# Where the first x of an MLP is loaded and scaled during attention, in a fused attention and MLP kernel: six head pairs instead of five

## The chip, the cores and the metric

One core of a Trainium2 chip runs the whole kernel. The metric is device time in microseconds: 708.55 us is the median of three runs (708.1 to 709.25).

## The reference

Attention over 4 batches, 8 heads, 576 positions and head size 64, with a bias that a small network makes from the distance of two positions; then an MLP over the 2304 tokens with model size 512 and inner size 2048.

```python
scores = scale * np.matmul(q, k.transpose(0, 1, 3, 2))
psi_rel = np.log1p(np.abs(rel))                      # rel = i - j
psi_i = np.log1p(np.maximum(pos[:, None], 1.0))
x = (psi_rel / psi_i)[..., None]
h = np.maximum(x @ w1 + b1, 0.0)
scores = scores + (h @ w2).transpose(2, 0, 1)[None]
scores = scores - np.max(scores, axis=-1, keepdims=True)
attn = np.exp(scores)
attn = attn / (np.sum(attn, axis=-1, keepdims=True) + 1e-09)
x = np.matmul(attn, v)        # then (batch, position, head * size), 2304 x 512
h = x @ w_in
g = np.where(h > 0.0, h, np.exp(np.minimum(h, 0.0)) - 1.0)
out = g @ w_out
```

## The kernel before

The order of the instructions on each engine is written out by hand. There are three stages: the bias of all heads, attention, and the MLP.

**Attention** goes over 16 head pairs n (4 batches of 4 pairs). A pair has five units i = 0 to 4, for the query blocks u = 0, 1, 4, 2, 3 (`order`). In a unit TensorE makes the scores of both heads into two PSUM banks each (line 291, S in `STEPS`), VectorE adds the bias and takes the row minimum (line 303, X), ScalarE takes the exponential (line 314), TensorE transposes the result of the unit before (line 355, T), and two copies bring each transposed block to SBUF (line 359): the second copy (r = 1) is VectorE's for even u and ScalarE's for odd u. TensorE also makes the weighted sums of v of the pair before (line 399). They go out to DRAM unscaled (`xd`, lines 409 to 412). At the second unit of pairs 4, 8 and 12 the row sums of the batch before are inverted (lines 324 and 325), at the fourth they are transposed and sent to DRAM (`rd`, line 333).

All loads and stores of this stage are issued by SP in one queue in program order: the next pair's k and q at the end of unit 0 (lines 99 to 105), one raw block of MLP weights in unit 2 (line 250), v in unit 3 (line 111). Each pair also decodes one block of MLP weights, given as 64-bit floats: VectorE (lines 259, 263, 265) and GpSimd (lines 255, 268), stored at line 270. The first of these VectorE steps, line 259, comes once in each pair, in its second unit.

**The first x of the MLP.** `early` is a table of what else is done in the last pairs; its key (n - 16, i) names a pair and the unit at whose end it happens. `load_x(0, r, h)` fetches the weighted sums of half the channels (r) for 384 tokens (h) with `xd` DMAs (line 448) into `xr` and, for each, two DMAs that spread the inverted sums over partitions (line 452) into `rr`, which has one buffer: three DMAs where the tokens lie in one piece (h = 0), nine where they lie in three pieces (h = 1). `scale_x` multiplies the two on VectorE (line 460). `high_x` (line 483) and `low_x` (line 486) split the result into two parts for TensorE (B11, B12, B21, B22), `sums_x` (line 474) makes sums for the fast matrix product.

**The MLP** works on 3 blocks of 768 tokens; for each it goes over 8 blocks of the inner size. The first two (i = 0, 1) are plain products (`eight`), the others a seven-product scheme (`seven`) whose left operands are sums of the weights, made by `make_w(i)`. This generator's steps are placed by `at(i, k, ...)`, into the k-th product of block i. The second matmul (line 723) adds into six PSUM banks; when one is complete, VectorE or ScalarE copies it to an `os` tile (line 732, three buffers) and SP sends it out (line 734).

Of the kernel before, what the change touches and what calls it, by code (L numbers as in the profile page):

```python
# [10 lines left out]
F32 = mybir.dt.float32  # L11
# [13 lines left out]
def kernel(  # L25
# [11 lines left out]
    nc = tc.nc  # L37
    B, HP, D, _, S = qT.shape
    NT, DM = out.shape
    H = 2 * HP  # L40
    P = 128
# [37 lines left out]
    def w_bank(name):  # L79
        return wp.tile([P, 512], F32, tag="w", name=name)  # L80
# [8 lines left out]
    NP = len(pairs)  # L89
# [253 lines left out]
    def trans_p(n, u):  # L343
        pta, ptb = st["pt", n]

        ss = st["ss", n, u]
        if u < NCH:
            dst, o = (pta, u * P) if u < 2 else (ptb, (u - 2) * P)
            banks = [w_bank("wt") for r in range(2)]
            for x in range(2 * NCH):  # L350
                e, j = divmod(x, NCH)
                c = e * (S + TAIL) + j * P
                for r in range(2):
                    q = slice(r * TAIL, (r + 1) * TAIL)
                    nc.tensor.transpose(banks[r][:, x * TAIL:(x + 1) * TAIL], ss[q, c:c + P], ident[q, q])  # L355
            for r in range(2):
                d = dst[:, 0:2 * NCH, o + r * TAIL:o + (r + 1) * TAIL]
                copy = nc.vector.tensor_copy if r == 1 and u % 2 == 0 else nc.scalar.copy
                copy(d, banks[r].rearrange("p (x t) -> p x t", t=TAIL))
                yield  # L360
        else:
            o = 2 * P
            M = NCH * TAIL
            banks = [w_bank("wt") for e in range(2)]
            for j in range(NCH + 1):
                for e, w in enumerate(banks):
                    r = slice(e * TAIL, (e + 1) * TAIL)
                    if j < NCH:
                        c = j * P
                        nc.tensor.transpose(w[:, j * TAIL:(j + 1) * TAIL], ss[r, c:c + P], ident[r, r])  # L370
                    elif e == 0:
                        nc.tensor.transpose(w[r, M:M + TAIL], ss[r, NCH * P:], ident[r, r])
                    else:
                        nc.tensor.transpose(w[:, M:M + TAIL], ss[r, S - P:], ident[r, r])
            for e, w in enumerate(banks):
                r = slice(e * TAIL, (e + 1) * TAIL)
                d = pta[:, e * NCH:(e + 1) * NCH, o:o + TAIL]
                nc.scalar.copy(d, w[:, 0:M].rearrange("p (j t) -> p j t", j=NCH))
                nc.scalar.copy(pta[r, 2 * NCH, o:o + TAIL], w[r, M:M + TAIL])
                yield  # L380
# [123 lines left out]
    xo = dict(zip(("B11", "B12", "B21", "B22"), slots))  # L504
# [5 lines left out]
    def attention():  # L510
# [17 lines left out]

        V, G = nc.vector, nc.gpsimd
        early = {  # L530
            (-5, 3): [(load_x, 0, 0, 0)],
            (-4, 1): [(scale_x, 0, 0, 0, V)],
            (-4, 2): [(load_x, 0, 0, 1)],
            (-4, 4): [(scale_x, 0, 0, 1, V)],
            (-3, 0): [(load_x, 0, 1, 0)],
            (-3, 1): [(high_x, 0, "B11", xo["B11"], V.tensor_copy)],
            (-3, 2): [(scale_x, 0, 1, 0, V)],
            (-3, 3): [(load_x, 0, 1, 1), (low_x, 0, "B11", xo["B11"], V)],
            (-2, 0): [(scale_x, 0, 1, 1, V)],
            (-2, 1): [(high_x, 0, "B12", xo["B12"], V.tensor_copy)],  # L540
            (-2, 2): [(low_x, 0, "B12", xo["B12"], V)],
            (-2, 3): [(high_x, 0, "B21", xo["B21"], V.tensor_copy), (sums_x, 0, ("T1",), G)],
# [25 lines left out]
        for n in range(NP):  # L568
# [4 lines left out]
            for i, u in enumerate(order):  # L573
                run = scores(n, u)
                back = trans_p(n, order[i - 1]) if i > 0 else trans_p(n - 1, order[-1]) if n > 0 else iter(())
                for op in STEPS[i]:
                    if op in ("S", "X"):
# [40 lines left out]
        for _ in trans_p(NP - 1, order[-1]):  # L618
            pass
# [10 lines left out]
    def mlp():  # L630
        ep = ctx.enter_context(tc.tile_pool(name="ep", bufs=3))
# [17 lines left out]
        FIRST = 2  # L649
# [13 lines left out]
        def make_w(i):  # L663
            q = i % NQ
            ta, tb = place_w(i, 0), place_w(i, 1)
            S1 = wq.tile([P, 4, AW], F32, tag="S", name="S")
            wa, wb = wab.pop(2 * q), wab.pop(2 * q + 1)
            A11, A12, A21, A22 = (w[:, k * AW:(k + 1) * AW] for w in (wa, wb) for k in range(2))
            hi, lo = AT[i][:, 0], AT[i][:, 1]
            flat = lambda t: t.rearrange("p a m -> p (a m)")  # L670
            v = nc.vector
            parts = [
                (flat(hi[:, 4:6]), flat(lo[:, 4:6]), wa[:, 0:DM]),
                (W2[i][:, 0, 0], W2[i][:, 1, 0], wa[:, DM:]),
                (hi[:, 6], lo[:, 6], A22),
                (W2[i][:, 0, 1], W2[i][:, 1, 1], wb[:, DM:]),
                (flat(hi[:, 0:4]), flat(lo[:, 0:4]), flat(S1)),
            ]
            high = lambda k: nc.scalar.copy(parts[k][0], parts[k][2])
            low = lambda k: v.tensor_sub(parts[k][1], parts[k][2], parts[k][0].bitcast(F32))  # L680
            yield
            v.tensor_add(S1[:, 0], A21, A22)
            v.tensor_sub(S1[:, 2], A11, A21)
            high(0)
            yield
            v.tensor_sub(S1[:, 1], S1[:, 0], A11)
            v.tensor_sub(S1[:, 3], A12, S1[:, 1])
            low(0)
            yield
            high(4)  # L690
            yield
            low(4)
            high(2)
            yield
            low(2)
            high(1)
            yield
            high(3)
            yield
            low(1)  # L700
            yield
            low(3)
            yield
            nc.sync.dma_start(out=wA[q], in_=ta.bitcast(F32))
            nc.sync.dma_start(out=wB[q], in_=tb.bitcast(F32))
# [4 lines left out]
        def second(i, order):  # L710
            j = i // NQ
            for e, h in order:
                gh, gl = g[i, e]
                wh, wl = (
                    [ws[2 * i + e][f][:, DM:] for f in range(2)] if i < FIRST else [W2[i][:, f, e] for f in range(2)]
                )
                for t in range(3 * h, 3 * h + 3):
                    if (j, t) not in acc:
                        acc[j, t] = accp.tile([P, DM], F32, tag="acc", name="acc")
                        count[j, t] = 0  # L720
                    for x, w in ((gh, wh), (gh, wl), (gl, wh)):
                        count[j, t] += 1
                        nc.tensor.matmul(  # L723
                            acc[j, t],
                            lhsT=x[:, t * P:(t + 1) * P],
                            rhs=w,
                            start=(count[j, t] == 1),
                            stop=(count[j, t] == 6 * NQ),
                        )
                        if count[j, t] == 6 * NQ:  # L730
                            os = ep.tile([P, DM], F32, tag="os", name="os")
                            (nc.scalar.copy if t % 2 else nc.vector.tensor_copy)(os, acc[j, t])  # L732
                            t0 = 2 * j * HB + t * P
                            nc.sync.dma_start(out=out[t0:t0 + P, :], in_=os)
                        yield


# [98 lines left out]
        def at(i, k, fn, *args):  # L836
            plans.setdefault((i, k), []).append((fn, args))

        V, G = nc.vector, nc.gpsimd
# [11 lines left out]
        for i in range(FIRST, NQ + FIRST):  # L851
            q = i % NQ
            run = make_w(i)
            for e in range(2):
                at(i - 2, 0 if i - 2 < FIRST else 2, load_w, 2 * q + e, wq if i % 2 == 0 else keep)
            for k in (0, 1, 1, 2, 2, 3, 3) if i == FIRST else (0, 1, 2, 3, 4, 5, 6):
                at(i - 1, k, next, run)
            at(i, 0, next, run)
            at(i, 1, next, run)
            at(i, 3, next, run, None)  # L860
# [53 lines left out]
    with tc.manual_schedule():  # L914
        make_identity(nc, ident)
        bias_phase()
        attention()
        ph1.close()
        ps1.close()
        mlp()  # L920
# [58 lines left out]
```

## Time and profile before

| | |
|---|---|
| median of 3 runs | 708.55 us |
| the profiled execution, its own time | 708.4 us |
| its span, first to last instruction | 706.6 us |
| mean granted TensorE clock | 0.994 |
| TensorE matmul, busy | 679.3 us (96%) |
| VectorE, busy | 470.7 us (67%) |
| ScalarE, busy | 440.6 us (62%) |
| GpSimd, busy | 75.3 us (11%) |
| attention, first raw weights used to the MLP's first product | 68.75 to 319.47 us |

The engines are named PE (TensorE's matmuls), PEld (its weight loads), DVE (VectorE), ACT (ScalarE), POOL (GpSimd) and SP. Lines of a timeline begin with the start and the duration in microseconds; instructions of a kind that follow each other are merged, with their count behind an x. A bracket at the end tells how long the engine was idle before, and what ended it. The share of busy time is a mean over the three stages; what a change in one place is worth is read from the waits there.

### The profile page before, as it was taken

The page shows a single profiled execution, that of the slowest core. Times are in us where ns is not written, and L with a number is a line of the kernel's source. Part 1 is how long each engine was busy: PE and PEld are TensorE (multiplying, and loading weights), DVE is VectorE, ACT ScalarE, POOL GpSimd, SP SyncE. Part 2 cuts the span into 40 slices and gives each one's busy share as a digit, 9 for nine tenths or more (in the row PEclk, how much of TensorE's full clock was granted, in tenths as well). Part 3 has the DMA queues.
Part 4 walks back from the last instruction along what each step waited for, and adds up shares of the span by engine and source line. Part 5 has one row for each costly group of instructions (what it writes and reads, how often), then busy time and mean ns, then how long its engine had stood idle before and what let it go on. Part 6 is the DMA issues. An engine that isn't in the chain of part 4 may idle for free.

```text
span 706.6 us, 13181 instructions
## 1 busy us (share of the span) xinstructions
PE 679.3 (96%) x4992; PEld 508.7 (72%) x4992; DVE 470.7 (67%) x948; ACT 440.6 (62%) x953; POOL 75.3 (11%) x104
## 2 busy tenths in 40 slices
PE   5997999999999979899999999999999999999997
PEld 3434555555555545458799988999988899988896
DVE  6995767767766757875777899854456754444443
ACT  6996787787877757675665667643444644434433
POOL 0001332322233212330000000000000000000000
PEclk9999999999999999999999999999999999999999
DMA  6998655456555766625379977898684455555202
GB/s 165 222 221 210 219 176 200 159 163 205 185 187 185 222 175 195 216 103 187 81 268 333 330 260 257 317 350 310 212 306 176 164 209 212 202 207 214 88 1 89
DMA packets 49934, 144.58 MB, mean 205 GB/s; under 512 B 13376, under 2 KB 26448, under 8 KB 42192
## 3 DMA queue, kind: packets, MB, share of 16 engines
q1 hardware_dynamic: 49136, 143.44, 60.9%
q8 instruction: 39, 0.64, 0.4%
q10 hardware_dynamic: 736, 0.31, 0.2%
q14 instruction: 23, 0.19, 0.1%
HBM read 92.14 MB, written 40.97 MB: 188 GB/s over the span
## 4 chain that ended last, share of the span: by engine, by line
PE 51%; issue 1%; DVE 1%; ACT 1%; DMA 0%; SPq 0%; ACTq 0%
PE acc L723 27%; PE h L772 24%; DVE bias L497 0%; DMA out_dram<-os 0%; DVE e L751 0%; ACT e L758 0%; ACT gh L752 0%; DVE xs L486 0%; ACT bias L493 0%; DVE gl L746 0%; ACT e L757 0%; ACT xs L483 0%; DVE os L732 0%; DMA wf<-da 0%; ACT os L732 0%
## 5 line engine op out<-in xcount | busy, mean ns | idle before, releaser
L723 PE MATMUL acc<-wB,gh 128*128 128x512 f32 x528 | 171.3, 392 | 0.0
L303 DVE CUSTOM_DVE_ANT_0 ss<-ps,bias 128x576 f32<-128x576 f32 x128 | 91.8, 754 | 58.9 <-PE ps L291 50.2
L314 ACT ACTIVATE ss<-ss,nm 128x576 f32<-128x576 f32 x128 | 98.2, 769 | 36.9 <-DVE nm L303 36.4
L291 PE MATMUL ps<-kk,qq 64*128 64x288 f32 (+1 forms) x640 | 110.2, 423 | 7.9 <-DVE nm L303 7.6
L772 PE MATMUL h<-bias 128*128 128x384 f32 x552 | 111.8, 339 | 0.8 <-DVE rs L332 0.5
L723 PEld LDWEIGHTS acc<-wB,gh 128*128 128x128 f32 x528 | 98.1, 188 | 14.3
L772 PEld LDWEIGHTS h<-bias 128*128 128x128 f32 x552 | 99.6, 188 | 9.0 <-DVE e L751 1.9
L723 PE MATMUL acc<-wB,gl 128*128 128x512 f32 x264 | 103.8, 393 | 0.0
L291 PEld LDWEIGHTS ps<-kk,qq 64*128 64x128 f32 (+1 forms) x640 | 63.3, 178 | 28.2 <-DVE nm L303 12.5
L752 ACT CAST gh<-e 128x384 fp32r<-128x384 f32 x96 | 49.4, 514 | 44.8 <-DVE e L751 44.2
L757 ACT ACTIVATE e<-c 128x384 f32<-128x384 f32 x66 | 34.7, 525 | 53.4 <-DVE c L803 53.4
L746 DVE TENSOR_TENSOR gl<-e,gh 128x384 fp32r<-128x384 f32 x96 | 53.2, 554 | 18.1 <-ACT gh L752 15.8
L772 PE MATMUL h<-bias,wA 128*128 128x384 f32 x276 | 56.3, 338 | 0.9 <-issue 0.9
L751 DVE SCALAR_TENSOR_TENSOR e<-e,c 128x384 f32<-128x384 f32 x66 | 36.7, 557 | 30.1 <-ACT e L758 29.9
L757 ACT ACTIVATE e<-h 128x384 f32<-128x384 f32 x28 | 13.8, 491 | 68.3 <-PE h L772 68.3
L193 PE MATMUL bps<-rel,cs 128*32 128x288 f32 x576 | 45.5, 430 | 10.7 <-ACT rel L183 7.8
L723 PEld LDWEIGHTS acc<-wB,gl 128*128 128x128 f32 x264 | 49.5, 187 | 7.8
L399 PE MATMUL wv<-pta,vv 128*64 128x320 f32 (+1 forms) x320 | 54.4, 454 | 0.0
L772 PEld LDWEIGHTS h<-bias,wA 128*128 128x128 f32 x276 | 50.1, 188 | 5.0 <-issue 1.4
L758 ACT ACTIVATE e<-e 128x384 f32<-128x384 f32 x96 | 50.5, 526 | 3.0
L355 PEld LDWEIGHTS wt<-ident,ss 64*128 64x128 f32 x1024 | 37.5, 139 | 19.6 <-issue 13.0
L803 DVE TENSOR_TENSOR c<-h,u 128x384 f32<-128x384 f32 x66 | 36.7, 556 | 20.1 <-PE h L772 20.1
(105 smaller groups left out, 924.6 us busy)
## 6 DMA issues: line engine op xcount, KB each, us to landing
wB<-wB SPq DMA_DIRECT2D x22, 1024.0 KB, 5.0
raw<-in_wd_dram SPq DMA_DIRECT2D x16, 1024.0 KB, 11.0
bias<-wA SPq DMA_DIRECT2D x9, 1792.0 KB
wA<-wA SPq DMA_DIRECT2D x8, 1792.0 KB
wa<-wf SPq DMA_DIRECT2D x20, 512.0 KB, 4.3
bias<-bo SPq DMA_DIRECT2D x16, 576.0 KB, 6.4
wA<-bias SPq DMA_DIRECT2D x5, 1792.0 KB, 10.7
wf<-da SPq DMA_DIRECT2D x16, 512.0 KB, 3.9
```

The lines of the kernel that those rows point to most:

```text
L193: nc.tensor.matmul(ps[32 * g:32 * g + 32, f, 0:HS], lhsT=W2, rhs=rel[g][:, f * HS:(f + 1) * HS], start=True, stop=True,)
L291: nc.tensor.matmul(banks[e][:, f, 0:HS] if u < NCH else banks[0][r, f, 0:HS], lhsT=qq[r, rows], rhs=kk[r, f * HS:(f + 1) * HS], start=True ...
L303: nc.vector.tensor_tensor_reduce(out=s.rearrange("p (f x) -> p f x", f=2), in0=ps[:, :, 0:HS], in1=bap.rearrange("p (f x) -> p f x", f=2), ...
L314: nc.scalar.activation(s, s, AF.Exp, bias=nm[:, e:e + 1], scale=-1.0, accum_out=sm[:, hp, col:col + 1])
L355: nc.tensor.transpose(banks[r][:, x * TAIL:(x + 1) * TAIL], ss[q, c:c + P], ident[q, q])
L399: nc.tensor.matmul(w[e * D:(e + 1) * D, 0:N], lhsT=l, rhs=r, start=(j == first), stop=(j == end))
L723: nc.tensor.matmul(acc[j, t], lhsT=x[:, t * P:(t + 1) * P], rhs=w, start=(count[j, t] == 1), stop=(count[j, t] == 6 * NQ),)
L746: nc.vector.tensor_sub(gl, t, gh.bitcast(F32))
L752: nc.scalar.copy(g[i, e][0][:, h * HB:(h + 1) * HB], t)
L757: nc.scalar.activation(t, src, AF.Relu, scale=-1.0)
L758: nc.scalar.activation(t, t, AF.Exp, scale=-1.0)
L772: nc.tensor.matmul(ps, lhsT=a[f][c], rhs=x[y][c], start=(start and k == 0), stop=(stop and k == len(todo) - 1), skip_group_check=not start,)
```

## The change

Four edits:

1. In the last pair (n = 15) VectorE makes the second copy of a transposed block for odd u too.
2. The four loads of the MLP's first x and their scalings move to pairs 9 to 13. Each scaling comes about one pair after its load. The split of B11 keeps its pair; its second half comes one unit earlier. What follows from pair 14 on stays.
3. The `os` tile gets four buffers instead of three, and the outputs of odd t are issued by ScalarE's queue instead of SP's.
4. The steps of `make_w(2)` go to other products of block 1: before, products 0 to 3 took 1, 2, 2 and 2 steps; now they take 2, 1, 1 and 3. The first step of the generator issues nothing.

```diff
-                copy = nc.vector.tensor_copy if r == 1 and u % 2 == 0 else nc.scalar.copy
+                copy = nc.vector.tensor_copy if r == 1 and (u % 2 == 0 or n == NP - 1) else nc.scalar.copy
...
-            (-5, 3): [(load_x, 0, 0, 0)],
-            (-4, 1): [(scale_x, 0, 0, 0, V)],
-            (-4, 2): [(load_x, 0, 0, 1)],
-            (-4, 4): [(scale_x, 0, 0, 1, V)],
-            (-3, 0): [(load_x, 0, 1, 0)],
+            (-7, 3): [(load_x, 0, 0, 0)],
+            (-6, 3): [(scale_x, 0, 0, 0, V)],
+            (-6, 4): [(load_x, 0, 0, 1)],
+            (-5, 4): [(scale_x, 0, 0, 1, V), (load_x, 0, 1, 0)],
+            (-4, 4): [(scale_x, 0, 1, 0, V), (load_x, 0, 1, 1)],
             (-3, 1): [(high_x, 0, "B11", xo["B11"], V.tensor_copy)],
-            (-3, 2): [(scale_x, 0, 1, 0, V)],
-            (-3, 3): [(load_x, 0, 1, 1), (low_x, 0, "B11", xo["B11"], V)],
-            (-2, 0): [(scale_x, 0, 1, 1, V)],
+            (-3, 2): [(low_x, 0, "B11", xo["B11"], V)],
+            (-3, 4): [(scale_x, 0, 1, 1, V)],
             (-2, 1): [(high_x, 0, "B12", xo["B12"], V.tensor_copy)],
...
-                            os = ep.tile([P, DM], F32, tag="os", name="os")
+                            os = ep.tile([P, DM], F32, tag="os", name="os", bufs=4)
                             (nc.scalar.copy if t % 2 else nc.vector.tensor_copy)(os, acc[j, t])
                             t0 = 2 * j * HB + t * P
-                            nc.sync.dma_start(out=out[t0:t0 + P, :], in_=os)
+                            (nc.scalar if t % 2 else nc.sync).dma_start(out=out[t0:t0 + P, :], in_=os)
...
-            for k in (0, 1, 1, 2, 2, 3, 3) if i == FIRST else (0, 1, 2, 3, 4, 5, 6):
+            for k in (0, 0, 1, 2, 3, 3, 3) if i == FIRST else (0, 1, 2, 3, 4, 5, 6):
```

## Rows read from the trace of the kernel before

**Rows 1.** Page part 1: busy time of each engine.

```profile
PE 679.3 (96%) x4992; PEld 508.7 (72%) x4992; DVE 470.7 (67%) x948; ACT 440.6 (62%) x953; POOL 75.3 (11%) x104
```

**Rows 2.** Timelines of DVE and PE, pairs 12 and 13.

```profile
261.09 0.96 DVE L460 TENSOR_TENSOR xr<-xr,rr 128x768 f32<-128x768 f32 x1 [5.12 <-DMA rr<-rd]
...
262.78 2.96 PE L291 MATMUL ps<-kk,qq 64*128 64x288 f32 x8 [3.89 <-DVE nm L303]
...
284.51 0.96 DVE L460 TENSOR_TENSOR xr<-xr,rr 128x768 f32<-128x768 f32 x1 [4.08 <-DMA xd<-xs]
```

**Rows 3.** Windows: busy time per engine, PEclk, DMA share, GB/s.

```profile
264.00:266.00 2.00, 2.00 (x9) 1.06 (x7) 0.79 (x3) 1.67 (x5) 0.24 (x1) 0.50 0.90 249
```

**Rows 4.** Timeline of DVE, line 259, in pairs 8, 9, 12, 13, 14, 15.

```profile
184.06 0.69 DVE L259 TENSOR_SCALAR dm<-raw 128x1024 int32<-128x1024 uint32 x1
...
199.62 0.69 DVE L259 TENSOR_SCALAR dm<-raw 128x1024 int32<-128x1024 uint32 x1
...
245.23 0.70 DVE L259 TENSOR_SCALAR dm<-raw 128x1024 int32<-128x1024 uint32 x1
...
266.57 0.69 DVE L259 TENSOR_SCALAR dm<-raw 128x1024 int32<-128x1024 uint32 x1
...
286.75 0.69 DVE L259 TENSOR_SCALAR dm<-raw 128x1024 int32<-128x1024 uint32 x1
...
302.13 0.81 DVE L259 TENSOR_SCALAR dm<-raw 128x1024 int32<-128x1024 uint32 x1
```

**Rows 5.** Timeline of PE, start of the MLP.

```profile
337.06 2.37 PE L772 MATMUL h<-bias 128*128 128x384 f32 x12 [0.21 <-DVE e L751]
...
346.86 1.29 PE L772 MATMUL h<-bias,wA 128*128 128x384 f32 x6 [0.95 <-issue]
```

**Rows 6.** Timeline, end: the last output's copy.

```profile
702.94 0.59 ACT L732 COPY os<-acc 128x512 f32<-128x512 f32 x1 [0.78 <-DMA out_dram<-os]
```

**Rows 7.** Timeline of SP: pair 10 to 11 undisturbed, then a nine-DMA load.

```profile
224.22 0.47 SPq L99 DMA_DIRECT2D kk<-in_k_dram  x1
...
226.63 1.23 SPq L105 DMA_DIRECT2D qq<-in_q_dram  x2
...
234.06 0.34 SPq L250 DMA_DIRECT2D raw<-in_wd_dram  x1
...
252.17 0.78 SPq L448 DMA_DIRECT2D xr<-xd  x1
...
257.37 1.23 SPq L452 DMA_DIRECT2D rr<-rd  x2
```

**Rows 8.** Timeline of DVE, pair 10 to 11: gaps before two reductions.

```profile
222.53 0.76 DVE L303 CUSTOM_DVE_ANT_0 ss<-ps,bias 128x576 f32<-128x576 f32 x1 [0.44 <-ACT ss L314]
...
225.17 0.76 DVE L303 CUSTOM_DVE_ANT_0 ss<-ps,bias 128x576 f32<-128x576 f32 x1 [0.41 <-PE ps L291]
```

**Rows 9.** Timelines of POOL and DVE: decoding and the copies of B11, B12.

```profile
231.38 1.12 POOL L255 TENSOR_SCALAR da<-raw 128x1024 f32<-128x1024 f32 x1
...
270.04 0.55 DVE L483 CAST bias<-xr 128x768 fp32r<-128x768 f32 x1
...
288.09 1.11 POOL L255 TENSOR_SCALAR da<-raw 128x1024 f32<-128x1024 f32 x1
...
288.35 1.27 DVE L483 CAST bias<-xr 128x768 fp32r<-128x768 f32 x1
```

**Rows 10.** DMA issues of one line: count, size, median us to landing.

```profile
qq<-in_q_dram SPq DMA_DIRECT2D x32, 144.0 KB, 2.9
```

**Rows 11.** Timeline of PE, pair 11's end: the next pair's first scores.

```profile
239.03 1.43 PE L291 MATMUL ps<-kk,qq 64*128 64x288 f32 x8
```

**Rows 12.** Timelines of PEld and PE, pair 15.

```profile
309.12 0.78 PEld L291 LDWEIGHTS ps<-kk,qq 64*128 64x128 f32 x6 [0.31 <-DVE nm L303]
...
316.84 1.95 PE L399 MATMUL wv<-ptb,vv 128*64 128x256 f32 x16 [0.58 <-ACT ptb L359]
```

## The prediction

> **What bounds the kernel now.** I read page part 1 first: TensorE is busy for 96% of the span, VectorE for 67%, ScalarE for 62% [rows 1]. So a saving exists only where TensorE waits, and the timelines of VectorE and TensorE show where. In the last head pairs VectorE comes to a scaling of x whose load hasn't landed. It stands 5.12 us in pair 12 and 4.08 us in pair 13, and TensorE, which needs VectorE to empty its score banks, stops 3.89 us behind the first [rows 2]. The windows add what TensorE's busy time hides: after that stop the granted clock is 0.50, the lower level of 1.2 GHz [rows 3], and eight score matmuls take 2.96 us [rows 2].
>
> The measure of a pair is a fixed step of it, the first decoding multiply of VectorE (line 259) [rows 4]. From pair 9 to pair 12 it moves 45.61 us, 15.20 a pair. Pair 8, which also inverts a batch's sums, as pair 12 does, takes 15.56. Pairs 12, 13 and 14 take 21.34, 20.18 and 15.38, together 56.90 where 15.56 + 2 x 15.20 = 45.96 would do. This excess, 10.94 us, is all that better-placed loads can give back in attention; it includes the slow clock. Everything behind attention is the MLP, where TensorE hardly waits: 0.21 and 0.95 us near its start [rows 5]. At the end the last output copy waits 0.78 us for a buffer [rows 6].
>
> **The loads and scalings.** Nothing is added or removed: four loads (3, 9, 3 and 9 DMAs on SP's queue) and four multiplies of 0.96 us on VectorE [rows 2] go to earlier pairs. A nine-DMA load took SP from 252.17 to 258.60, 6.43 us [rows 7], and its scaling could begin at 261.09 [rows 2], so 9 us after its first issue. Now each load has nearly a pair, 15.2 us, before its scaling. The two waits go, and the slow clock with them: -10.94.
>
> What comes back, by the gaps into which the multiplies now fall:
> - First scaling, pair 10, third unit's end: VectorE has a gap of 0.44 us there before the reduction that frees the banks for the next scores [rows 8]. A multiply of 0.96 overruns by some 0.4 to 0.5, and TensorE's scores follow directly. Bounds 0 and 0.5; I take 0.4, as that reduction is what TensorE waits for next.
> - The other three stand behind a pair's last copy. The gap before the next pair's first reduction is 0.41 [rows 8], the overrun again 0.5; but there TensorE has weighted sums and transposes to do before the scores that need these banks. Bounds 0 and 0.5 each; I take 0.1 each, 0.3.
> - Pair 13's copy of B11 stays in its second unit, but VectorE reaches it on time now, while GpSimd runs its decoding multiply in that very place (231.38 in pair 11) [rows 9]. The copy took 0.55 us when it came late in pair 13, and 1.27 in pair 14, where it began 0.26 after GpSimd's multiply [rows 9]. Pair 14, with such a copy, is 0.18 over 15.20 [rows 4]. So 0.2 for pair 13 (bounds 0 and 0.7), and pair 14's 0.2 stays.
>
> The sum of the part: -10.94 + 0.4 + 0.3 + 0.2 + 0.2 = -9.9, between -10.7 and -8.0.
>
> The Trainium skill (SBUF — State Buffer, Who interferes with whom) says that VectorE in a two-port mode and GpSimd take one shared pair of ports as an exclusive lock, and the later one blocks completely. The trace agrees: the 1.27 us copy ended 0.42 us after GpSimd did. By this rule B11's copy becomes some 0.7 us longer and the sum is as above; without it, it would be 0.2 lower.
>
> What is queued behind the moved DMAs on SP: the nine-DMA loads now stand at the end of pairs 10 and 12, right before the loads of the next pair's k and q, which in an undisturbed pair are issued from 224.22 to 227.86 [rows 7]. With 6.4 to 7.1 us in front (and, in pair 12, up to 1 us for the row tile that the scaling in the same place must give back) they end at 234 to 236. q lands 2.9 us after its issue [rows 10], at 237 to 239, and TensorE begins the next pair's scores at 239.03 [rows 11]. So it is just hidden: 0 to 2 us are left. Next is the raw weight load, due at 234.06 [rows 7], when VectorE has released its buffer: 0 to 2 us late, with 11 us until its first reader at 245.23 [rows 4]; I cost it at nothing. If this cover fails, the first rival is what happens.
>
> **The last pair's copies.** In pair 15 the second copies of units 1 and 3 go from ScalarE to VectorE. At the pair's end TensorE waits 0.58 us for two copies that ScalarE makes one after the other [rows 12]; side by side they give 0.4 of it (bounds 0 and 0.58). In the third unit the copy comes in front of reductions for which TensorE already waits (0.31 us [rows 12]); VectorE there also splits B22, so the copy, some 0.6 us, passes on. Bounds 0 and 0.7, taken 0.6, the nearest row being that wait. Sum +0.2, between -0.5 and +0.7.
>
> **The first weights' sums.** The steps for block 2 keep their count; two VectorE subtractions and a ScalarE copy come one step earlier, the long copy-and-subtract pair is spread. In the trace VectorE and ScalarE wait for each other there, and TensorE's 0.95 us stop before the first product of block 2 is for a bank that VectorE frees late [rows 5]. I expect that stop to go, and the earlier one of 0.21 to grow by the two operations now ahead of it, 0.6 to 0.7 us: -0.95 + 0.65 = -0.3. Bounds: both go (-1.2), or one stays and the other grows (+0.6).
>
> **The outputs.** With a fourth buffer the last copy waits for the tile four outputs back instead of three. Outputs follow each other every 0.7 us, so its 0.78 us wait [rows 6] goes but for 0.1: -0.7, between -0.8 and -0.4. The second queue itself I cost at nothing: SP only issues there. A DMA issue in ScalarE's stream, in the first two token blocks, lies in an engine that is 62% busy over the span [rows 1]; bounds 0 and 0.3 for each of the two, taken 0.
>
> **Sum.** 708.4 - 9.9 + 0.2 - 0.3 - 0.7 = 697.7 against the profiled execution's own time; the median of the runs is 0.15 above that execution, so **697.8 us**.
>
> **Rivals.**
> - q comes late. The q load issued in pair 11 or 13, pushed back by nine DMAs, lands 1 to 3 us after TensorE wants it, without loss of clock. For it: the slack is 0 to 2 us by the rows above. Against it: the DMAs that stood behind nine others in pair 12 delayed nothing that the trace shows. Time: 697.8 + 1 to 4 for one or both, 699 to 702.
> - A scaling still waits, so the change doesn't do what it says for one of the two large loads: pair 12's excess of 5.78 (21.34 - 15.56) or pair 13's 4.98 stays, 702.8 to 703.6. Against it: 15 us for a load that needed 9.
> - Slower: both nine-DMA loads hold up q so long that TensorE stops at two pair heads and its clock falls both times. The price of one such stop is pair 12's excess, 5.78 us for a VectorE wait of 5.12. Two of them cost 11.6 and make 709.4; from 5.4 us per head on, the gain of 10.9 is gone. That needs q to be issued 6 to 8 us later than I have it, nine DMAs in some 13 us instead of 6.43. Nothing in the rows does that, except that more transfers may now meet at a pair's end.
>
> **How the numbers follow.** My forecast has 0.76; q late 0.13; a scaling that waits 0.06; slower 0.05. The forecast's own bounds: -10.7 - 0.5 - 1.2 - 0.8 below, -8.0 + 0.7 + 0.6 - 0.4 above, so 695.4 to 701.4; all terms at one end together are unlikely, so 695.8 below, and 701.2 above, which takes in most of the q rival too. Left out are the rival of the waiting scaling, the slower one, part of the q rival, and the forecast's tails. A measurement tells 0.2%, 1.4 us, from no change: faster 0.94, same 0.01, slower 0.05.
>
> **What will show it.** Right: no VectorE wait before line 460 in attention; line 259's steps 15.2 apart from pair 8 to 15 except 15.6 in 8 and 12; granted clock 1.00 throughout pair 12; the first scores of pairs 12 and 14 without a DMA in front; the last copy waiting under 0.2 us. The copy term shows in pair 15's third unit, the weights' sums in TensorE's first two waits in the MLP. Wrong: a wait of TensorE for kk or qq, a wait of VectorE for raw, a clock of 0.50 behind either, or ScalarE waiting behind an output DMA in the first two token blocks.

## The result, and the profile after

The changed kernel takes 695.67 us (median of four runs, 695.08 to 697.41) where the kernel before takes 708.52 beside it: a ratio of 0.9822, 95% interval 0.9801 to 0.9842. Predicted were 697.8 us, between 695.8 and 701.2. So it is 12.85 us faster where 10.75 were forecast. That is the lower edge of the range: the median lies 0.13 us below it, the mean of the four runs, 695.96, just inside.

Line numbers behind line 358 may differ by one from those of before. Page part 1 of the changed kernel:

```profile
PE 677.7 (98%) x4992; PEld 510.3 (74%) x4992; DVE 472.2 (68%) x950; ACT 439.6 (63%) x951; POOL 76.3 (11%) x104
```

TensorE's share rises from 96% to 98% [rows 1] with the same busy time; what went is idle time and slow clock. Where it went is read by the marks of the prediction. VectorE's timeline, line 259 in pairs 8, 9, 12, 13, 14 and 15 [rows 4]:

```profile
182.28 0.69 DVE L259 TENSOR_SCALAR dm<-raw 128x1024 int32<-128x1024 uint32 x1
...
197.85 0.69 DVE L259 TENSOR_SCALAR dm<-raw 128x1024 int32<-128x1024 uint32 x1
...
243.80 0.69 DVE L259 TENSOR_SCALAR dm<-raw 128x1024 int32<-128x1024 uint32 x1
...
259.37 0.69 DVE L259 TENSOR_SCALAR dm<-raw 128x1024 int32<-128x1024 uint32 x1
...
274.75 0.69 DVE L259 TENSOR_SCALAR dm<-raw 128x1024 int32<-128x1024 uint32 x1
...
290.16 0.80 DVE L259 TENSOR_SCALAR dm<-raw 128x1024 int32<-128x1024 uint32 x1
```

From pair 8 to pair 15 there are now 107.88 us instead of 118.07. Pairs 12, 13 and 14, which took 21.34, 20.18 and 15.38, take 15.57, 15.38 and 15.41. The scalings and the copies of B11 and B12, again from VectorE's timeline:

```profile
220.23 0.95 DVE L460 TENSOR_TENSOR xr<-xr,rr 128x768 f32<-128x768 f32 x1
...
238.44 0.95 DVE L460 TENSOR_TENSOR xr<-xr,rr 128x768 f32<-128x768 f32 x1
...
253.83 0.95 DVE L460 TENSOR_TENSOR xr<-xr,rr 128x768 f32<-128x768 f32 x1
...
260.97 1.28 DVE L483 CAST bias<-xr 128x768 fp32r<-128x768 f32 x1
...
269.47 0.95 DVE L460 TENSOR_TENSOR xr<-xr,rr 128x768 f32<-128x768 f32 x1
...
276.35 1.30 DVE L483 CAST bias<-xr 128x768 fp32r<-128x768 f32 x1
```

No line has a bracket: no scaling waits any more [rows 2]. The copy of B11, 0.55 us in pair 13 before, takes 1.28 as that of B12 does [rows 9]. The granted clock is 1.00 in every window of 2 us from 236 to 308 us; here is a row from pair 12, where it was 0.50 (PEclk is the third number from the end) [rows 3]:

```profile
252.00:254.00 2.00, 2.00 (x27) 1.32 (x24) 2.00 (x6) 1.90 (x6) 0.00 (x0) 1.00 0.99 373
```

The queue of SP at the end of pair 10, and TensorE's first scores of pair 12, which need what it issues, with the weighted sums behind them:

```profile
222.40 0.43 SPq L448 DMA_DIRECT2D xr<-xd  x1
...
227.39 1.23 SPq L452 DMA_DIRECT2D rr<-rd  x2
...
230.77 1.24 SPq L105 DMA_DIRECT2D qq<-in_q_dram  x2
...
232.75 0.36 SPq L250 DMA_DIRECT2D raw<-in_wd_dram  x1
```

```profile
237.60 1.43 PE L291 MATMUL ps<-kk,qq 64*128 64x288 f32 x8
238.96 1.30 PE L399 MATMUL wv<-pta,vv 128*64 128x320 f32 x8
```

The nine DMAs stand ahead of k and q [rows 7], q's last issue ends at 232.01, 3.42 us behind pair 11's line 259, and TensorE's scores start without a wait [rows 11]. The raw block is issued 4.16 us behind line 259 where it was 4.03 before (234.06 and 230.03), so it is not late either. TensorE's waits in pair 15 and at the start of the MLP, with block 2's first product at the end [rows 12, 5]:

```profile
297.07 1.91 PE L291 MATMUL ps<-kk,qq 64*128 64x288 f32 x8 [0.32 <-DVE nm L303]
...
305.11 1.95 PE L399 MATMUL wv<-ptb,vv 128*64 128x256 f32 x16 [0.33 <-DVE sm L324]
...
325.81 2.37 PE L771 MATMUL h<-bias 128*128 128x384 f32 x12 [0.84 <-DVE e L750]
...
334.29 1.23 PE L771 MATMUL h<-bias,wA 128*128 128x384 f32 x6
```

The stop of 0.95 us ahead of block 2 is gone, and that of 0.21 has become 0.84. At the end of pair 15 TensorE waits 0.33 us instead of 0.58; the profile names VectorE's instruction right behind its copy. At the end of the kernel, the last matmul of the last tile and the last two output copies [rows 6]:

```profile
688.93 0.69 DVE L731 COPY os<-acc 128x512 f32<-128x512 f32 x1 [0.85 <-DMA out_dram<-os]
689.00 0.39 PE L722 MATMUL acc<-wB,gl 128*128 128x512 f32 x1
689.56 0.59 ACT L731 COPY os<-acc 128x512 f32<-128x512 f32 x1 [0.90 <-DMA out_dram<-os]
```

The bracket of the last copy is longer than before, 0.90 us. It is ScalarE's whole idle time, though: the last matmul ends at 689.39, so the copy is 0.17 us late. Waiting for a buffer still costs 0.17 us there, not 0.90. In the kernel before the last matmul ended at 702.00 and the last copy began at 702.94 [rows 6], 0.94 us late:

```profile
701.61 0.39 PE L723 MATMUL acc<-wB,gl 128*128 128x512 f32 x1
```

**All stretches of all kernels.** The same marks cut every profiled execution into stretches: line 259 of pair 8; from there to pair 15; on to the MLP's first product; on to block 2's first product; first to last output copy; and everything from pair 8 to the end. T2 is how long behind the MLP's first product VectorE's first subtraction there begins (line 474). From block 2 to the first of the last output copies it is 351.73 to 351.85 us in all of them.

| kernel | pair 8 at | 8 to 15 | to the MLP | T2 | to block 2 | copies | from 8 on |
|---|---|---|---|---|---|---|---|
| before | 184.06 | 118.07 | 17.34 | 7.27 | 27.39 | 4.30 | 522.5 |
| changed | 182.28 | 107.88 | 17.58 | 7.11 | 26.55 | 3.53 | 511.0 |
| loads only | 184.74 | 107.89 | 17.33 | 7.33 | 27.44 | 4.29 | 512.4 |
| old loads | 182.30 | 118.84 | 17.58 | 7.23 | 26.65 | 3.52 | 522.0 |
| one copy | 184.51 | 107.88 | 17.06 | 6.63 | 26.08 | 3.51 | 510.0 |
| old steps | 185.51 | 107.89 | 17.59 | 6.55 | 26.66 | 3.53 | 511.2 |
| one queue | 184.21 | 107.88 | 17.58 | 6.78 | 26.23 | 3.54 | 510.7 |
| three buffers | 184.83 | 107.91 | 17.58 | 7.57 | 27.01 | 4.31 | 512.3 |
| early store | 184.85 | 107.88 | 17.58 | 2.05 | 25.13 | 3.52 | 509.6 |
| eighteen | 183.13 | 117.61 | 17.58 | 6.71 | 26.16 | 3.52 | 520.4 |
| fifteen | 183.38 | 113.26 | 17.58 | 6.75 | 26.20 | 3.51 | 516.2 |
| combined | 183.92 | 107.52 | 17.07 | 2.05 | 25.12 | 3.51 | 508.7 |
| splits | 182.81 | 107.17 | 17.08 | 2.04 | 25.14 | 3.52 | 508.4 |

Stretches repeat well where the code is the same (107.88 to 107.91). The first column doesn't: no edit touches anything up to pair 8, and yet it varies by 3.2 us. The times of single runs vary by as much, so small effects are read from the stretches.

### The profile page after: what moved, and what is told of

The parts are those of the page before. It is cut to its first block, busy times and chain, and to the rows that moved or that the text cites. A ratio compares the mean times of both kernels' runs of the same rounds, so it can differ in the third digit from the quotient of the medians.

```text
span 693.3 us, 13183 instructions
## 1 busy us (share of the span) xinstructions
PE 677.7 (98%) x4992; PEld 510.3 (74%) x4992; DVE 472.2 (68%) x950; ACT 439.6 (63%) x951; POOL 76.3 (11%) x104
## 4 chain that ended last, share of the span: by engine, by line
PE 92%; DMA 3%; DVE 2%; issue 1%; ACT 1%; SPq 0%; ACTq 0%; DVEq 0%
PE acc L722 28%; PE h L771 24%; PE wv L399 13%; PE ps L291 12%; PE bps L193 7%; PE wt L355 5%; PE wm L340 2%; DMA raw<-in_wd_dram 1%; PE wt L370 1%; DMA T<-in_rtab_dram 1%; DVE ss L303 0%; DVE bias L497 0%; DMA out_dram<-os 0%; DVE e L750 0%; ACT os L731 0%
## 5 line engine op out<-in xcount | busy, mean ns | idle before, releaser
L291 PE MATMUL ps<-kk,qq 64*128 64x288 f32 (+1 forms) x640 | 108.1, 419 | 1.8 <-DVE nm L303 1.6
L193 PE MATMUL bps<-rel,cs 128*32 128x288 f32 x576 | 48.1, 423 | 7.7 <-ACT rel L183 7.7
```

The source lines that it names most:

```text
L193: nc.tensor.matmul(ps[32 * g:32 * g + 32, f, 0:HS], lhsT=W2, rhs=rel[g][:, f * HS:(f + 1) * HS], start=True, stop=True,)
L291: nc.tensor.matmul(banks[e][:, f, 0:HS] if u < NCH else banks[0][r, f, 0:HS], lhsT=qq[r, rows], rhs=kk[r, f * HS:(f + 1) * HS], start=True ...
```

## The experiments

**Each edit alone or left out.** Loads only: the kernel before with the new table `early`. Old loads: the changed kernel with the old table.

> The kernel before with the new places of loads and scalings alone. Theory: attention from the line 259 of pair 8 to that of pair 15 shrinks from 118.07 us to 107.9 as in the changed kernel, and nothing else moves: 17.3 us from there to the MLP's first product, 27.4 us to block 2's first product, 4.3 us between the first and the last output copy. The 1.8 us by which the changed kernel was earlier at pair 8 is chance of one execution. Time 708.5 - 10.2 = 698.3 us, ratio 0.9856. Rival: those 1.8 us at the start belong to the loads (they change something ahead of pair 8); then pair 8 is at 182.3 again and the time is 696.5 us, ratio 0.983.

Measured: 698.03 us, ratio 0.9846 (0.9824 to 0.9867), and 107.89 us from pair 8 to 15; the rest as before within 0.05. Pair 8 is at 184.74, not at 182.3: the theory holds, its rival falls.

> The changed kernel with loads and scalings at their old places; the last pair's copies, the outputs and the sums' steps stay changed. Theory: the waits of 5.1 and 4.1 us and the clock of 0.50 are back, 118.1 us from pair 8 to pair 15; what is left of the gain is +0.24 (copies) - 0.84 (sums) - 0.77 (outputs) = -1.4, so 707.1 us, ratio 0.998. Rival: the 1.8 us at the start belong to one of these three edits (a fourth buffer or other moves where tiles lie); then 705.3 us, ratio 0.9955, and pair 8's line 259 is at 182.3 instead of 184.1.

Measured: 706.74 us, ratio 0.9971 (0.9953 to 0.9989). Here pair 8 does come at 182.30, but the early store below, which has all three of these edits too, has it at 184.85, so the early start isn't theirs. The waits are back, from VectorE's timeline:

```profile
259.55 0.96 DVE L460 TENSOR_TENSOR xr<-xr,rr 128x768 f32<-128x768 f32 x1 [5.34 <-DMA rr<-rd]
...
283.50 0.96 DVE L460 TENSOR_TENSOR xr<-xr,rr 128x768 f32<-128x768 f32 x1 [3.82 <-DMA xd<-xs]
```

From pair 8 on this kernel is 0.5 us shorter than before and not 1.4, since the waits cost 0.8 more this time (118.84).

What varies at the start: windows of the changed kernel and of the kernel with old steps, from 40 to 50 us, in the bias stage (the last number is GB/s).

```profile
40.00:50.00 10.00, 10.00 (x128) 4.54 (x128) 10.00 (x24) 10.00 (x17) 0.00 (x0) 1.00 1.01 236
```

```profile
40.00:50.00 10.00, 9.15 (x128) 3.19 (x120) 10.00 (x25) 10.00 (x17) 0.00 (x0) 1.00 0.99 221
```

The changed kernel's DMAs move 236 GB/s there, those of the other 221. They reach pair 8 at 182.28 and 185.51, the earliest and the latest of thirteen; the kernel before is the median. In this window the three earliest executions move 235 to 238 GB/s and all others 217 to 229, but among these the order isn't that of the rates (227 GB/s and 184.85 for the early store). So the DMAs are only a likely cause, and why they differ isn't known.

**The copies of the last pair.**

```diff
-... if r == 1 and (u % 2 == 0 or n == NP - 1) else nc.scalar.copy
+... if r == 1 and (u % 2 == 0 or n == NP - 1 and u == 3) else nc.scalar.copy
```

> The changed kernel, but in the last pair only the copy at the pair's end (u = 3) goes to VectorE; that of the third unit (u = 1) stays ScalarE's. Theory: the third unit's copy on VectorE delays the reductions for which TensorE waits, the one at the end shortens a wait, so this kernel has the gain without the loss: the stretch from line 259 of pair 15 to the MLP's first product falls from 17.58 to some 17.0 to 17.1 us, time 695.2, ratio to the changed kernel 0.9992. Rival: the third unit's copy costs nothing and 17.58 stays; the time is the changed kernel's.

Measured: 695.32 us, ratio to before 0.9804 (0.9784 to 0.9823); the stretch to the MLP is 17.06 us. So the third unit's copy costs 17.58 - 17.06 = 0.52 and the pair-end copy gives 17.33 - 17.06 = 0.27 (against loads only). The matmuls' wait of 0.32 us for line 303 in pair 15 is gone; the weight loads there wait 0.32 for it, as they did before (0.31 [rows 12]).

**The steps of the first weights' sums**: `(0, 0, 1, 2, 3, 3, 3)` back to `(0, 1, 1, 2, 2, 3, 3)`.

> The changed kernel with the old places of the steps of the first weights' sums. Theory: the stop of 0.95 us ahead of block 2 is back and the earlier one falls from 0.84 to 0.2 us; from the MLP's first product to block 2's first product 27.4 us instead of 26.55, so 0.8 us more, 696.5 us. Rival: block 2's start depends on when the data of VectorE's T2 come rather than on these steps; then 26.5 us stay and the time is the changed kernel's.

Measured: 697.17 us (ratio to before 0.9829, 0.9809 to 0.985), and only 26.66 us to block 2, 0.11 more than in the changed kernel. But the stop is back in TensorE's timeline as expected:

```profile
337.65 1.28 PE L771 MATMUL h<-bias,wA 128*128 128x384 f32 x6 [0.97 <-issue]
```

The theory's number (27.4) is missed, and its rival, that block 2's start hangs on VectorE's T2, is half right. In the table "to block 2" less T2 is 20.11 to 20.12 in the three kernels with the old steps (27.39 - 7.27, 27.44 - 7.33, 26.66 - 6.55) and 19.42 to 19.45 in all with the new steps whose T2 is late. So the steps give 0.67 us whatever T2 does, and between 6.55 and 7.57 us every 0.1 us of T2 is 0.1 us of block 2. The kernel with old steps lost 0.67 and had T2 0.56 earlier by chance.

**What T2 waits for.** The chain of work that ended last, from the end of pair 15 on, in the changed kernel (start, duration, what):

```profile
308.75 0.34 SPq L490
...
309.19 0.68 DMA wf<-da
309.86 4.98 issue
314.85 0.09 DVE T L474
```

VectorE's T2 stands behind the landing of `wf<-da`, the store of the last decoded weights (line 270), which SP issues behind the fourth weight load. They share no data; by the kernel's pools, T2's tile is placed in memory that the stage before gives up, the decoding's tiles among it. The chain has "issue" ahead of T2 here; in the kernel with eighteen DMAs (below, where line 474 is 477) the bracket names the store:

```profile
325.03 0.96 DVE L477 TENSOR_TENSOR T<-xr,xr 128x768 f32<-128x768 f32 x1 [4.58 <-DMA wf<-da]
```

So the store goes forward:

```diff
+        decode(dp, plan.get(NP - 1), "store")
         late += pv(NP - 1, 0, (0, 1, 2, 3, 4), xp)
...
         low_w(2, nc.vector)
-        decode(dp, plan.get(NP - 1), "store")
```

> The changed kernel, but the store of the last decoded block of weights (line 270) is issued ahead of the last weighted sums instead of behind the fourth weight load. Theory: VectorE's first work in the MLP (T2, line 474) stands behind that store's landing, and every stop of TensorE up to block 2 is VectorE's lateness from there. The store now starts when GpSimd has finished the block, some 3 us before the MLP's first product, and lands 5 to 6 us later; T2 then begins 2 to 3 us after the first product instead of 7.1, the stop of 0.84 us goes, and from the first product to block 2's it takes 25.5 us instead of 26.55: 1.0 us less, 694.6 us. Rival: T2 waits for something else that comes 7 us after the first product, or the stop is for ScalarE's part; then 26.5 us stay.

Measured: 695.17 us (ratio 0.9814, 0.979 to 0.9838). SP's store, VectorE's T2 and block 2's first product in the timelines of three engines:

```profile
307.07 0.32 SPq L270 DMA_DIRECT2D wf<-da  x1
```

```profile
312.36 0.94 DVE L474 TENSOR_TENSOR T<-xr,xr 128x768 f32<-128x768 f32 x1
```

```profile
335.44 1.23 PE L771 MATMUL h<-bias,wA 128*128 128x384 f32 x6
```

T2 follows VectorE's work without a wait, 2.05 us behind the MLP's first product (310.31), block 2 starts after 25.13 us, 1.42 earlier, and TensorE has no wait on the way (25.5 us were expected). So in the changed kernel all its stops between the MLP's first product and block 2 come from that store. In the times of whole runs 1.4 us can't be told from their spread; here they are 0.5 us below the changed kernel's, in another set of runs.

**The outputs.** One queue: all outputs on SP's queue, four buffers. Three buffers: `bufs=4` taken out, two queues.

> The changed kernel with all outputs on SP's queue again; the os tile keeps four buffers. Theory: the gain at the end comes from the fourth buffer alone, so from the first to the last output copy of the last block it takes 3.5 us as in the changed kernel (4.3 before). Rival: it is the second queue, since SP issues an output only every 0.7 us or more and its issues follow each other late; then 4.0 to 4.3 us.

> The changed kernel with three buffers for the os tile and outputs on two queues. Theory (the buffer): 4.3 us from the first to the last output copy of the last block, as before. Rival (the queue): 3.5 us, as in the changed kernel.

Measured, one run each: 696.69 us with one queue, where the copies take 3.54 us, and 698.92 with three buffers, where they take 4.31. ScalarE's last copy but one with three buffers:

```profile
692.11 0.59 ACT L731 COPY os<-acc 128x512 f32<-128x512 f32 x1 [1.66 <-DMA out_dram<-os]
```

With three buffers this copy begins 1.66 us after ScalarE's last work and waits for an output to land, as in the kernel before (1.67), and all copies behind it are late. The buffer is the whole gain, the second queue nothing. The Trainium skill (Trainium Kernel Development and Optimization, Key Constraints) says that issuing from several engines saves only the time of issuing, as all use the same DMA engines; the runs with one queue and with two agree, 3.54 and 3.53 us.

**How much later q could come.** Eighteen: in the two large loads each DMA split by channel block. Fifteen: only those into `rr`.

```diff
...
-                nc.sync.dma_start(
-                    out=rr[e * D:(e + 1) * D, :, done:done + m],
-                    in_=rows[:, o:o + m].partition_broadcast(D),
-                )
+                for c in cs:
+                    nc.sync.dma_start(
+                        out=rr[e * D:(e + 1) * D, c, done:done + m],
+                        in_=rows[c, o:o + m].partition_broadcast(D),
+                    )
...
```

> The changed kernel with each nine-DMA load split into eighteen, by channel block; the same bytes, about 6 us more of issuing ahead of the next pair's k and q in pairs 11 and 13. Theory: the cover is short. In the changed kernel q's last issue ends at 232.0 and, 3 us to landing, is there 2.6 us before TensorE needs it at 237.6 (pair 12), and about 1.2 us before in pair 14. 6 us more make it 3.5 and 5 us late; TensorE waits for qq both times, and the time is 704 us, up to 709 if the granted clock falls behind each stop. Rival: DMAs of half the size are issued so much faster, or SP has so much room, that TensorE's scores never wait; then no wait for qq, and the changed kernel's time.

Measured: 706.08 us, ratio 0.9958 (0.994 to 0.9975). TensorE's waits at the heads of pairs 12 and 14, and a window behind the first:

```profile
239.94 2.89 PE L291 MATMUL ps<-kk,qq 64*128 64x288 f32 x8 [1.33 <-DMA qq<-in_q_dram]
...
275.90 0.72 PE L291 MATMUL ps<-kk,qq 64*128 64x288 f32 x2 [1.24 <-DMA qq<-in_q_dram]
...
277.72 1.94 PE L291 MATMUL ps<-kk,qq 64*128 64x288 f32 x6 [1.10 <-DMA qq<-in_q_dram]
```

```profile
242.00:244.00 2.00, 2.00 (x8) 0.65 (x9) 1.53 (x4) 1.09 (x3) 0.65 (x1) 0.50 0.81 229
```

Counted from line 259 of the pair before, q's last issue ends 5.36 us later in pair 11 and 4.06 in pair 13, and the scores begin 1.48 and 1.40 us later. So for the first scores 3.9 and 2.7 us of delay were free, more than the 2.6 and 1.2 expected. In pair 14 TensorE waits a second time, for the other half of q. The steps, though, are 20.22 and 20.09 us instead of 15.21 and 15.38: behind the stop of 1.33 us the granted clock is at 0.50, the lower of its two levels, as it is behind those of pair 14 (279 to 281 us), and the price is 5.0 us in pair 12 and 4.7 in pair 14.

> The changed kernel with only the row tiles of the two large loads split, fifteen DMAs instead of nine: some 3.0 to 3.5 us more of issuing ahead of k and q. Theory: with eighteen DMAs q was issued 5.4 us later in pair 11 and TensorE began 1.5 us late, so 3.9 us of delay are free there; in pair 13 its two halves were 4.1 us later and TensorE 1.4 and 2.7 us late, so 1.4 us are free. So now no wait for qq at pair 12, its step 15.2 us; at pair 14 a wait of 0.5 to 1.5 us, and, if a stop of that length already costs the clock (1.33 us cost 5.0 in all with eighteen DMAs), a step of 18 to 20 us instead of 15.4. Rival: a stop costs what it lasts; then pair 14's step is 16 to 17 us. Second rival: the delay of q grows with DMA traffic, not with SP's issues, and pair 12 waits too.

Measured: 701.37 us in one run. TensorE's waits, with the weighted sums behind the first scores; line 259 of pair 12; and a window behind the head of pair 12 and of pair 14 (PEclk third from the end):

```profile
239.06 0.72 PE L291 MATMUL ps<-kk,qq 64*128 64x288 f32 x2 [0.19 <-DMA qq<-in_q_dram]
...
240.14 1.21 PE L291 MATMUL ps<-kk,qq 64*128 64x288 f32 x6 [0.37 <-DMA qq<-in_q_dram]
241.28 1.30 PE L399 MATMUL wv<-pta,vv 128*64 128x320 f32 x8
...
272.74 0.72 PE L291 MATMUL ps<-kk,qq 64*128 64x288 f32 x2 [1.41 <-DMA qq<-in_q_dram]
```

```profile
246.38 0.69 DVE L259 TENSOR_SCALAR dm<-raw 128x1024 int32<-128x1024 uint32 x1 [0.18 <-DMA raw<-in_wd_dram]
```

```profile
240.00:242.00 2.00, 1.86 (x12) 1.18 (x14) 1.45 (x4) 0.73 (x4) 1.75 (x2) 1.00 0.85 193
274.00:276.00 2.00, 2.00 (x10) 0.80 (x8) 1.26 (x3) 0.41 (x1) 1.37 (x1) 0.51 0.84 238
```

Pair 12, where no wait was expected, has two of 0.19 and 0.37 us: q is 4.2 us later and 3.9 are free, so the bound was right and the forecast of the delay (3.0 to 3.5) too small. The second rival named a wait in pair 12, but its cause isn't needed: the delay is one of SP's issues, and as much of it is free as with eighteen DMAs. The clock stays at 1.00, and the step is 16.68, 1.47 more. The two brackets show only 0.56 of that. By the starts, TensorE lost 1.21 us: the weighted sums begin 11.58 us behind line 259 of pair 11 (229.70) where they begin 10.37 behind it in the changed kernel (238.96 and 228.59). The other 0.26 is line 259 of pair 12 itself, which now waits for its raw block, one of the prediction's signs of being wrong; in the changed kernel it doesn't wait. In pair 14 the waits are 1.41 and 0.15, the clock falls to 0.51, and the step is 19.34, 3.96 more. So a stop that left the clock at 1.00 cost TensorE the 1.21 us that it lost by the starts, and the stops behind which it fell cost two to four times their waits (5.0 for 1.33, 4.7 for 1.24 and 1.10, 3.96 for 1.41 and 0.15). The rival without the clock falls.

**A better version.** Combined: one copy and the early store, as above, and the first scaling at the end of pair 10.

```diff
-            (-6, 3): [(scale_x, 0, 0, 0, V)],
-            (-6, 4): [(load_x, 0, 0, 1)],
+            (-6, 4): [(scale_x, 0, 0, 0, V), (load_x, 0, 0, 1)],
```

> The changed kernel with three further edits: in the last pair only the pair-end copy on VectorE, the early store of the last decoded block, and the first scaling one unit later, at the end of pair 10, behind the pair's last copy like the other three. Theory: line 259 of pair 15 to the MLP's first product 17.06 us (from 17.58), from there to block 2's first product 25.1 (from 26.55), and the step from pair 10 to pair 11 15.2 (from 15.54), as a scaling at a pair's end cost nothing in pairs 11 and 12. From pair 8's line 259 to the end 508.7 us, where the changed kernel has 511.0; with a start as it has been in the other executions, 693.4 us. Rival for the scaling: the place costs 0.3 wherever it is, since VectorE's gap is 0.4 everywhere; then 15.5 stay. Rival for the rest: with VectorE no longer late, ScalarE's work comes up as the next wait ahead of block 2 and 25.1 isn't reached.

Measured: 694.41 us, ratio 0.9795 (0.9772 to 0.9818); 508.7 us from pair 8 on, as worked out, and a step of 15.20 from pair 10 to 11. The median is 1.0 us above the 693.4 expected, less than the start varies. The scaling and the reduction behind it, from VectorE's timeline:

```profile
224.54 0.95 DVE L460 TENSOR_TENSOR xr<-xr,rr 128x768 f32<-128x768 f32 x1
225.40 0.75 DVE L303 CUSTOM_DVE_ANT_0 ss<-ps,bias 128x576 f32<-128x576 f32 x1
```

VectorE is busy there without a gap, and TensorE doesn't notice, as it has weighted sums and transposes first.

Splits: the copies of B11 and B12 one unit earlier still.

```diff
-            (-3, 1): [(high_x, 0, "B11", xo["B11"], V.tensor_copy)],
+            (-3, 0): [(high_x, 0, "B11", xo["B11"], V.tensor_copy)],
...
-            (-2, 1): [(high_x, 0, "B12", xo["B12"], V.tensor_copy)],
+            (-2, 0): [(high_x, 0, "B12", xo["B12"], V.tensor_copy)],
```

> The combined kernel with the copies of B11 and B12 (line 483) one unit earlier, at the end of the pair's first unit, where VectorE stands idle for 1.6 us ahead of its next reduction; their second halves stay. Theory: the 0.18 and 0.20 us over 15.20 in pairs 13 and 14 are these two copies: beside GpSimd's decoding multiply they take 1.28 and 1.30 us where 0.55 would do, and VectorE has no gap for that behind. In the new place a copy may still be held up by GpSimd's add (2.4 us), but until no later than 0.1 us behind the time of the next reduction. So both steps become 15.20 to 15.25, 0.35 us less in all, 508.3 from pair 8 to the end, 694.0 us. Rival: the excess is the second halves' (line 486) or the scaling's; then 15.38 and 15.40 stay and the time is the combined kernel's.

Measured: 694.11 us, ratio 0.9797 (0.9771 to 0.9824). By the ratio it can't be told from the combined kernel (0.9795); by the stretches it is the fastest, 508.4 us from pair 8 on, 2.6 less than the changed kernel. The steps are 15.20 and 15.21: the excess was the copies'. B11's copy and GpSimd's add beside it:

```profile
256.25 1.58 DVE L483 CAST bias<-xr 128x768 fp32r<-128x768 f32 x1
```

```profile
255.04 2.37 POOL L268 TENSOR_TENSOR da<-da,dm 128x1024 int32<-128x1024 int32 x1
```

The copy takes 1.58 us, longer than in its old place, and ends 0.42 us behind GpSimd's add. It costs nothing now, as VectorE has the time there. This fits what the prediction cited of the Trainium skill (SBUF — State Buffer, Who interferes with whom): the later one is blocked for the whole of the other's instruction.

## Why the prediction was right, point by point

- **Loads and scalings**, -9.9: right, -10.19. Both waits and the slow clock behind the first went, all 10.94 us, and loads only shows that nothing else took part. (The terms of this part add up to -9.84, which was carried on as -9.9.) The first scaling cost 0.34 (0.4 predicted), pair 13 with B11's copy 0.18 and pair 14 0.21 (0.2 each). The three scalings at pair ends cost 0.0, not 0.3: that term ought to have been nothing, as its own reason (TensorE has other work there) said.
- **The cover of k and q**, 0 to 2 us left: right in kind, too short in size. 3.9 and 2.7 us were left ahead of the first scores. SP ended q's issues 3.42 us behind line 259 of pair 11, where the 234 to 236 us of the prediction are 4 to 6 behind it (230.03 in before).
- **The last pair's copies**, +0.2: right, +0.24, by both its parts: +0.52 in the third unit (0.6), -0.27 at the end (0.4).
- **The first weights' sums**, -0.3: right in how the steps act, too small in size. The one stop went, the other grew by 0.63 as forecast (0.65). But the steps gave 0.67 at equal T2, and 0.16 more came from T2, which happened to be earlier in this execution. I sized the lost stop by its bracket, 0.95. By the starts of matmuls it was 1.11: the last one ahead of it started at 345.52 and block 2's product at 346.86, 1.34 us apart, where it is 0.23 in the changed kernel (334.06 and 334.29). And from the stop ahead to that last matmul it took 8.46 us (337.06 to 345.52) where it now takes 8.25 (325.81 to 334.06), two delays too short for a bracket. The stop ahead now ends 18.07 us behind the MLP's first product instead of 17.59 (325.81 and 307.74, 337.06 and 319.47): -1.11 - 0.21 + 0.48 = -0.84, of which T2 is the 0.16. What the prediction did not have is the late event behind both stops: with the store early neither is there, and block 2 comes 1.42 us sooner.
- **The outputs**, -0.7: right, -0.77. The last copy began 0.94 us behind the last matmul and now begins 0.17 behind it; its bracket of 0.78, from which the term was taken, left out what the fourth copy's wait had already cost. The second queue is worth nothing, as costed, and ScalarE's issues in the first two token blocks cost nothing: from block 2 to the last outputs it is 351.75 us with one queue and 351.74 with two.
- **The sum.** From pair 8 on, -10.19 + 0.24 - 0.84 - 0.77 and +0.04 elsewhere make -11.5 us (522.5 to 511.0), where -10.7 was forecast: the terms were 0.8 short, 0.3 in the scalings and 0.5 in the weights' sums. Ahead of pair 8, where nothing was changed, the changed kernel's profiled execution is another 1.8 us earlier, the earliest of all thirteen; kernels with the same edits start later, so that is chance of one execution. The medians' 12.85 us can't be divided like this, as the other executions have no stretches. Besides the start, the price of the old waits differs between executions: the kernel before, in its runs beside the experiments, took from 705.33 us (mean granted clock 0.995) to 711.8 (0.984). So the 1.3 us beyond the stretches stay open, and no term of the prediction allowed for either.
- **The rivals.** None occurred. The first, q late "without loss of clock", was wrong about its price: 1.3 us of wait cost 5.0. The slower one put the point where the gain of the loads is gone at q 6 to 8 us later than forecast. With eighteen DMAs q's last issue ends 8.8 us behind line 259 in both pairs, 2.8 to 4.8 later than the 4 to 6 of the forecast, and 0.5 us of that gain are left (118.07 to 117.61). So the point comes sooner than I had it: the cover was larger, up to 7.3 us behind line 259 (3.42 + 3.9) where I had 6.1 (239.03 - 2.9 - 230.03), but a stop of 1.33 us cost nearly what I had taken from one of 5.12.

## What to carry to other kernels

Cut the trace at fixed instructions and compare stretches: effects of 0.1 us can be read there, while the start alone moved the profiled executions by 3 us. When several small stops of one engine follow each other, look in the chain of work for the one late event behind them, here a store, instead of costing each stop by itself. Before DMAs are put ahead of others in a queue, work out the slack of what stands behind them, and don't price a TensorE stop by its bracket alone: look at the starts of the matmuls and at the granted clock behind it.

## What the runs showed of the hardware

- A TensorE stop's price depends on the clock that follows: waits of 0.19 and 0.37 us at one pair's head left the granted clock at 1.00 and cost TensorE 1.2 us; waits of 1.33 us at one head, and of 1.41 and 0.15 at another, were followed by 0.50 and 0.51 and cost 5.0 and 4.0 us. The wait alone doesn't tell which it will be: in pair 13 of the kernel before, two stops of 1.07 and 1.09 us left the clock at 1.00 in every window of 2 us from 270 to 304 us:

```profile
286.20 1.19 PE L291 MATMUL ps<-kk,qq 64*64 64x288 f32 x8 [1.07 <-DVE nm L303]
288.48 1.23 PE L399 MATMUL wv<-ptb,vv 64*64 64x256 f32 x8 [1.09 <-DVE xs L405]
```

- Splitting a large load from nine DMAs into eighteen with the same bytes raised SP's issuing from 6.2 us (222.40 to 228.62) to 11.2 (223.25 to 234.46): 0.69 and 0.62 us for each issue, so half the bytes made an issue hardly cheaper.
- A store can hold up an engine that doesn't read its data, here, by the kernel's pools, through the memory that it leaves: 5 us on VectorE, and 1.4 us from the MLP's first product to block 2's.
